# One value product for both head groups, and the softmax sums carried in the gathered tile

## The chip, the cores and the metric

The kernel runs on one core of a Trainium2 chip. The metric is device time in microseconds (us); the time of a kernel is the median of its runs. The profile is one execution taken by the hardware profiler. Engines: TensorE (PE; PEld is its weight load), VectorE (DVE), ScalarE (ACT), GpSimd (POOL), SyncE (SP, which issues nearly all loads here).

## The reference, cut to what matters

One decode step for 8 sequences: layer norm, attention over the last 1024 cached positions with 32 query heads on 8 key/value heads, a feed-forward branch that gates the result, and a residual.

```python
# B = 8, D = 512, Hq = 32, Hkv = 8, Sk = 4096, Dh = 128, W = 1024, F = 1792
xn = layernorm(x)
q = (xn @ wq) -> [B, Hq, 1, Dh]
k, v = k_cache[:, :, Sk-W:], v_cache[:, :, Sk-W:]    # 4 query heads share one kv head
p = softmax(q @ k.T * Dh**-0.5)
s = (p @ v).reshape(B, 1, Hq*Dh) @ wo
g = silu((gelu(xn @ w_gate) * (xn @ w_up)) @ w_down)
out = x + s * g
```

K and V of the window are 4.19 MB for one sequence (2.10 MB each), 33.6 MB of the 47.5 MB that the kernel reads.

## The kernel before, in words

The kernel is scheduled by hand: on each engine the instructions run in the order in which the program writes them. An instruction that waits for another engine holds up everything behind it on its own engine.

**Before the loop.** `wq` and the first K and V blocks are loaded; the layer norm is computed, `q` is projected (line 254) and spread into a block-diagonal stationary `qbd` (line 277). Constants are built: `sel` (line 213) selects, for one head group, the heads that belong to it; `neg_st` and `neg_mv` mask scores of foreign heads.

**Loads.** `slot` hands out eight slots of 16 KB a partition, each for one K or V block of one sequence, or for weights of the feed-forward and output projection. A load of a new block into a slot waits until the old one's last reader is done. Each block is loaded in two halves (line 83), one for each group of four kv heads (NG = 2). SyncE issues the loads in program order, with at most eight in flight: each waits for the landing of the eighth before it, besides its slot.

**The loop over the 8 sequences b** (lines 407 to 425) runs, in program order: loads of K for b+2 and V for b+1; `turn_k(b+1, 0)`; `softmax(b)`; `scores(b+1, 0)`; `gather(b-1)`; `turn_k(b+1, 1)`; `scores(b+1, 1)`; `turn_p(b)`; `values(b)`; `keep_o(b)`; and behind b = 4 `regroup(0)`.

- `turn_k(b, g)` (line 242): one transpose on VectorE in 32 x 32 blocks turns half of the K block into `kT`.
- `scores(b, g)` (lines 293 and 304): TensorE; for g = 0 first two mask matmuls, then 8 matmuls of 512 columns into `S`, [128 x 1024] in PSUM.
- `softmax(b)`: VectorE takes the maximum `mx` (line 314) and folds it twice (319, 321); ScalarE scales it into `nb` (324, four instructions) and takes the exponential into `P_sb` (326), whose accumulator writes the row sums to `sums[:, b]`.
- `turn_p(b)` (line 337): VectorE turns `P_sb` into `pT`.
- `values(b)` (line 348): TensorE, for each head group g 32 matmuls with 32 stationary columns and 128 moving columns of V. The chunk c goes to the column group t = c % 4, so that four partial sums for 32 heads lie on the 128 partitions of `O_ps`, [128 x 2 x 128].
- `keep_o(b)` (line 361): ScalarE copies `O_ps` to `O_sb`.
- `gather(b)` (lines 369 and 373): for each g one FP32 matmul with `sel` adds the four partial sums and picks the group's heads, into 128 columns of `o_ps`, and one more does the same with `sums[:, b]` into column 128.
- `regroup(q)` (lines 384 to 400), for four sequences at once: divide by the sums, spread, eight small matmuls `r_ps`, and a cast into `oT`.

**Behind the loop.** SyncE issues the loads of the feed-forward weights and `wo`; then `gather(7)`, `regroup(1)`, the gate and up matmuls `z_ps` and `u_ps` (459), GELU on ScalarE and VectorE (469 to 482), the down projection `f_ps` (488), the output projection `s_ps` (507, 128 matmuls in four blocks of 32, one for each megabyte of `wo`), and two VectorE instructions and a store for the result.

Of the kernel before, what the change touches and what calls it, by code (L numbers as in the profile page):

```python
# [11 lines left out]
FP32 = mybir.dt.float32  # L12
# [9 lines left out]
def kernel(  # L22
# [13 lines left out]
    nc = tc.nc  # L36

    B, Sq, D = A_x.shape
    Hkv, Sk, Dh = A_k_cache.shape[1], A_k_cache.shape[2], A_k_cache.shape[3]
# [6 lines left out]
    P = nc.NUM_PARTITIONS  # L46
    NK = D // P
    HG = 4
    NG = Hkv // HG
    C = W * HG // P  # L50
# [7 lines left out]
    keep = ctx.enter_context(tc.tile_pool(name="keep", bufs=1))  # L58
    two = ctx.enter_context(tc.tile_pool(name="two", bufs=2))
# [31 lines left out]
    k_sb, v_sb = {}, {}  # L91
# [4 lines left out]
    def load_v(b):  # L96
# [14 lines left out]
        out=ident,  # L111
        in_=ident,
# [13 lines left out]
        out=xpad,  # L126
        in_=xpad,
# [17 lines left out]
        out=xhat,  # L145
# [9 lines left out]
    with tc.tile_pool(name="ps_x", bufs=1, space=PSUM) as ps_x:  # L155
# [7 lines left out]
        for t in range(4):  # L163
# [4 lines left out]
                start=True,  # L168
                stop=True,
# [12 lines left out]
        out=hv,  # L182
        in_=hv,
# [7 lines left out]
        out=neg_st,  # L191
        in_=neg_st,
# [8 lines left out]
        out=neg_mv,  # L201
        in_=neg_mv,
# [10 lines left out]
    sel = consts.tile([P, NG, Hq], FP32, name="sel")  # L213
    nc.vector.memset(sel, 0.0)
    for g in range(NG):
        nc.vector.tensor_reduce(
            out=sel[:, g, g * qd : (g + 1) * qd],
            in_=ident.rearrange("p (t g h) -> p g h t", t=4, g=NG)[:, g],
# [5 lines left out]
        out=own, in_=ident.rearrange("p (i e) -> p e i", e=8), axis=AX.X, op=ALU.add  # L224
    )
    pick = consts.tile([P, 4 * NU], BF16, name="pick")
    with nc.allow_low_precision(reason="sums of zeros and a single one"):
        nc.vector.tensor_reduce(
            out=pick, in_=ident.rearrange("p (a e) -> p a e", e=8), axis=AX.X, op=ALU.add
# [20 lines left out]
    with tc.tile_pool(name="ps_q", bufs=1, space=PSUM) as ps_q:  # L250
        q_ps = [ps_q.tile([P, 512], FP32, name=f"q_ps{i}") for i in range(8)]
        for k in range(NK):
            for i in range(8):
# [4 lines left out]
                    start=(k == 0),  # L258
                    stop=(k == NK - 1),
# [19 lines left out]


    pT, S, P_sb, O_ps = {}, {}, {}, {}
    sums = keep.tile([P, B], FP32, name="sums")

    actx = ExitStack()
    ps_s = actx.enter_context(tc.tile_pool(name="ps_s", bufs=2, space=PSUM))
# [26 lines left out]
    def softmax(b):  # L312
        mx = two.tile([P, 1], FP32, name="mx")
        nc.vector.tensor_reduce(  # L314
            out=mx, in_=S[b].rearrange("p a c -> p (a c)"), axis=AX.X, op=ALU.max
        )

        m2 = two.tile([64, 1], FP32, name="m2")
        nc.vector.tensor_tensor(out=m2, in0=mx[0:64, :], in1=mx[64:128, :], op=ALU.max)
        m1 = two.tile([32, 1], FP32, name="m1")  # L320
        nc.vector.tensor_tensor(out=m1, in0=m2[0:32, :], in1=m2[32:64, :], op=ALU.max)  # L321
        nb = two.tile([P, 1], FP32, name="nb")
        for j in range(4):
            nc.scalar.mul(nb[32 * j : 32 * j + 32, :], m1, -inv)  # L324
        P_sb[b] = two.tile([P, C // 2, 32, 2], BF16, name="P_sb")
        nc.scalar.activation(  # L326
            out=P_sb[b].rearrange("p c i w -> p c w i"),
            in_=S[b].rearrange("p a (c w i) -> p (a c) w i", w=2, i=32),
            func=ACT.Exp,
            bias=nb,  # L330
            scale=inv,
            accum_out=sums[:, b : b + 1],
        )

    def turn_p(b):
        pT[b] = two.tile([P, C // 2, Hq, 2], BF16, name="pT")
        nc.vector.transpose(  # L337
            out=pT[b].rearrange("p c h w -> p (c h w)").bitcast(I32),
            in_=P_sb[b].rearrange("p c i w -> p (c i w)").bitcast(I32),
        )  # L340

    def values(b):
        O_ps[b] = ps_o.tile([P, NG, Dh], FP32, name="O_ps")
        for g in range(NG):
            vv = v_sb[b][:, g].rearrange("p (c d) -> p c d", d=Dh)
            for c in range(C):
                t = c % 4
                nc.tensor.matmul(  # L348
                    O_ps[b][32 * t : 32 * t + 32, g, :],
                    pT[b][:, c // 2, :, c % 2],  # L350
                    vv[:, c, :],
                    start=(c < 4),
                    stop=(c >= C - 4),
                )

    o_ps = {}
    O_sb = {}

    def keep_o(b):
        O_sb[b] = two.tile([P, NG, Dh], FP32, name="O_sb")  # L360
        nc.scalar.copy(out=O_sb[b], in_=O_ps[b])  # L361

    def gather(b):
        q = b % 4
        if q == 0:
            o_ps[b // 4] = ps_g.tile([P, Dh + 1], FP32, name="o_ps")
        o = o_ps[b // 4][32 * q : 32 * q + 32, :]
        for g in range(NG):
            nc.tensor.matmul(  # L369
                o[:, 0:Dh], sel[:, g, :], O_sb[b][:, g, :], start=(g == 0), stop=(g == NG - 1)  # L370
            )
        for g in range(NG):
            nc.tensor.matmul(
                o[:, Dh : Dh + 1],
                sel[:, g, :],
                sums[:, b : b + 1],
                start=(g == 0),
                stop=(g == NG - 1),
            )

    def regroup(q):

# [24 lines left out]
    for b in range(B):  # L407
        if b + 2 < B:
            load_k(b + 2)
        if b + 1 < B:  # L410
            load_v(b + 1)
            turn_k(b + 1, 0)
        softmax(b)
        if b + 1 < B:
            scores(b + 1, 0)
        if b >= 1:
            gather(b - 1)
        if b + 1 < B:
            turn_k(b + 1, 1)
            scores(b + 1, 1)  # L420
        turn_p(b)
        values(b)
        keep_o(b)
        if b == 4:
            regroup(0)
# [10 lines left out]
    for u in range(NU):  # L436
        if u % 2 == 0:
            pair = slot("wo_sb").rearrange("p (v j d) -> p v j d", v=2, d=D)
        t = pair[:, u % 2]
# [6 lines left out]
        wo.append(t)  # L446

    gather(B - 1)
    regroup(1)
    actx.close()  # L450
# [4 lines left out]
    for n, ws in (("z_ps", wgu[0]), ("u_ps", wgu[1])):  # L455
        ps = ps_f.tile([P, FT], FP32, name=n)
        for k in range(NK):
            for t in range(4):
# [4 lines left out]
                    start=(k == 0),  # L463
                    stop=(k == NK - 1),
# [6 lines left out]
        out=z2, in0=z2, scalar1=0.044715, scalar2=1.0, op0=ALU.mult, op1=ALU.add  # L471
# [11 lines left out]
        out=hT.rearrange("p j b -> p (j b)"), in_=h_bf.rearrange("p (y j) -> p j y", j=NJ)  # L483
    )
    f_ps = ps_f.tile([P, DT], FP32, name="f_ps")
    for j in range(NJ):
        for t in range(4):
# [4 lines left out]
                start=(j == 0),  # L492
                stop=(j == NJ - 1),
# [4 lines left out]
        out=g_sb, in0=g_sb, scalar1=0.5, scalar2=0.5, op0=ALU.mult, op1=ALU.add  # L498
# [5 lines left out]
    for u in range(NU):  # L504
        for j in range(8):
            for t in range(4):
# [4 lines left out]
                    start=(u == 0 and j == 0),  # L511
                    stop=(u == NU - 1 and j == 7),
# [7 lines left out]
        out=out_f.rearrange("b (t d) -> t b d", t=4), in_=out_sb[0 : P : RB, :]  # L520
# [31 lines left out]
```

## Time and profile before

| what | value |
|---|---|
| median of 3 runs | 121.2 us (121.13 to 121.26) |
| span of the profiled execution (first to last instruction) | 119.2 us |
| VectorE busy | 75.7 us, 63% of the span |
| TensorE busy | 70.9 us, 59% |
| ScalarE busy | 31.4 us, 26% |
| loads | 47.46 MB read, 398 GB/s over the span |
| value matmuls (line 348) | 512, 9.2 us busy |
| gather matmuls (line 369) | 32 rows, 5.4 us busy |
| exponential (line 326) | 8, 1390 ns each |
| `kT` transposes (line 242) | 16, 2286 ns each |

The span is the profiled execution's own time; no other time of that execution is given, and the runs' median is 2.0 us longer than it. In a row of the timeline the first number is the start in us from the span's start, the second the time until the end of the row, then engine, line, operation, output and inputs, their shapes and the count; in brackets is the idle time of the engine before it and what ended it. In the rows of 40 digits each digit is a fortieth of the span (2.98 us), in tenths; `PEclk` is the granted clock of TensorE, 9 being full.

### The profile page before, as it was taken

The numbers are of one execution on the slowest core, as the hardware profiler recorded it, in microseconds if no ns is written. First come the engines' busy times: TensorE is split into PE (matmuls) and PEld (weight loads), VectorE is DVE, ScalarE is ACT, GpSimd is POOL, SyncE is SP. The second block draws the span as 40 slices with busy tenths as digits, with TensorE's granted clock in tenths as the row PEclk, the third lists the DMA queues.
The fourth block names the chain that finished last, engine by engine and source line by source line (L and its number), as shares of the span: only waits on it lengthen the run. The fifth ranks groups of instructions, "written<-read, shape, count | busy, mean of one in ns | idle before, by whom it ended". The sixth has DMA issues, their size and how long they took to land.

```text
span 119.2 us, 2306 instructions
## 1 busy us (share of the span) xinstructions
PE 70.9 (59%) x992; PEld 37.9 (32%) x992; DVE 75.7 (63%) x101; ACT 31.4 (26%) x75; POOL 3.2 (3%) x10
## 2 busy tenths in 40 slices
PE   0000079971299498896969692875783547544370
PEld 0000033420034154453635451433452433143350
DVE  1000387969998999999999968949952241751000
ACT  0300240076500715144161700421618101100000
POOL 2000052000000000000000000000000000000000
PEclk9999999998559999999999999999999755555555
DMA  6898899999999999999999999999999999999930
GB/s 177 352 518 363 374 429 432 423 429 426 434 418 423 434 426 421 426 432 418 423 432 426 421 423 429 423 429 421 423 429 433 443 438 404 438 414 429 402 140 3
DMA packets 6110, 47.61 MB, mean 399 GB/s; under 512 B 716, under 2 KB 852, under 8 KB 1108
## 3 DMA queue, kind: packets, MB, share of 16 engines
q1 hardware_dynamic: 6084, 47.46, 94.7%
q8 instruction: 8, 0.13, 0.4%
q14 instruction: 2, 0.02, 0.0%
q10 hardware_dynamic: 16, 0.01, 0.0%
HBM read 47.46 MB, written 0.01 MB: 398 GB/s over the span
## 4 chain that ended last, share of the span: by engine, by line
DMA 78%; PE 9%; DVE 6%; ACT 2%; issue 1%; ACTq 1%; DVEq 0%; SPq 0%
DMA k_sb<-in_A_k_cache_dram 32%; DMA wo_sb<-in_A_wo_dram 20%; DMA v_sb<-in_A_v_cache_dram 16%; DMA x_sb<-in_A_x_dram 9%; PE q_ps L254 8%; DVE qbd L277 3%; ACTq L78 1%; DVE q_both L267 1%; ACT L154 1%; DVE q_both L264 1%; PE s_ps L507 1%; DVE stats L137 1%; DVE y L515 0%; ACT rstd L141 0%; DVE out_sb L517 0%
## 5 line engine op out<-in xcount | busy, mean ns | idle before, releaser
L304 PE MATMUL S_ps<-kT,qbd 128*128 128x512 bf16 x128 | 31.9, 393 | 14.8 <-DVE kT L242 11.3
L242 DVE STREAM_TRANSPOSE kT<-k_sb 128x2048 int32<-128x2048 int32 x16 | 36.5, 2286 | 1.6 <-DMA k_sb<-in_A_k_cache_dram 1.6
L304 PEld LDWEIGHTS <-qbd 128*128 128x128 bf16 x128 | 12.6, 99 | 30.8 <-issue 14.2
L324 ACT ACTIVATE nb<-m 32x1 f32<-32x1 f32 x32 | 6.4, 201 | 20.1 <-DVE m L321 19.8
L326 ACT ACTIVATE P_sb<-S_ps,nb 128x1024 bf16<-128x1024 f32 x8 | 11.1, 1390 | 0.3
L348 PE MATMUL O_ps<-v_sb,pT 128*32 128x128 bf16 x512 | 9.2, 227 | 2.6 <-DVE pT L337 2.6
L314 DVE TENSOR_REDUCE mx<-S_ps 128x1 f32<-128x1024 f32 x8 | 9.6, 1194 | 1.6 <-PE S_ps L304 1.6
L254 PE MATMUL q_ps<-wq_sb,xnR 128*128 128x512 bf16 x32 | 9.9, 485 | 0.5 <-ACT x_res L171 0.5
L348 PEld LDWEIGHTS <-pT 128*32 128x32 bf16 x512 | 7.7, 100 | 5.6 <-issue 3.0
L159 PE MATMUL xnT_ps<-ident,xhat 8*128 8x8 bf16 x4 | 0.3, 174 | 15.2 <-DVE xhat L144 15.2
L361 ACT COPY O_sb<-O_ps 128x256 f32<-128x256 f32 x8 | 3.0, 372 | 22.7 <-PE O_ps L348 22.7
L137 DVE BATCH_NORM_STATS2 stats<-x_sb 8x6 f32<-8x512 bf16 x1 | 0.7, 681 | 12.0 <-DMA x_sb<-in_A_x_dram 12.0
L337 DVE STREAM_TRANSPOSE pT<-P_sb 128x512 int32<-128x512 int32 x8 | 5.7, 711 | 3.4 <-ACT P_sb L326 3.3
L507 PE MATMUL s_ps<-wo_sb,oT 128*32 128x128 bf16 x128 | 4.4, 307 | 3.9 <-DMA wo_sb<-in_A_wo_dram 3.9
L369 PE MATMUL o_ps<-O_sb,sel 128*32 128x128 f32 x32 | 5.4, 297 | 0.9 <-ACT O_sb L361 0.9
L293 PE MATMUL S_ps<-neg_mv,neg_st 128*128 128x512 bf16 x16 | 4.8, 381 | 1.9 <-DVE q_both L264 1.9
L254 PEld LDWEIGHTS <-xnR 128*128 128x128 bf16 x32 | 3.8, 118 | 6.4 <-issue 3.9
L264 ACT CAST q_both<-q_ps 128x512 bf16<-128x512 f32 x6 | 3.0, 613 | 8.6 <-PE q_ps L254 8.6
L507 PEld LDWEIGHTS <-oT 128*32 128x32 bf16 x128 | 3.5, 136 | 4.9 <-issue 4.7
L159 PEld LDWEIGHTS <-xhat 8*128 8x128 bf16 x4 | 0.2, 113 | 15.2 <-DVE xhat L144 15.2
L515 DVE TENSOR_TENSOR y<-s_ps,g_sb 128x128 f32<-128x128 f32 x1 | 0.3, 292 | 7.4 <-PE s_ps L507 7.4
L369 PEld LDWEIGHTS o_ps<-O_sb,sel 128*32 128x32 f32 x32 | 3.0, 115 | 4.0 <-issue 2.5
(64 smaller groups left out, 53.9 us busy)
## 6 DMA issues: line engine op xcount, KB each, us to landing
k_sb<-in_A_k_cache_dram SPq DMA_DIRECT2D x16, 1024.0 KB, 16.5
v_sb<-in_A_v_cache_dram SPq DMA_DIRECT2D x16, 1024.0 KB, 19.8
wq_sb<-in_A_wq_dram SPq DMA_DIRECT2D x1, 4096.0 KB, 12.2
wo_sb<-in_A_wo_dram SPq DMA_DIRECT2D x3, 1024.0 KB, 25.0
wgu_sb<-in_B_w_gate_dram SPq DMA_DIRECT2D x1, 1792.0 KB, 21.3
wgu_sb<-in_B_w_up_dram SPq DMA_DIRECT2D x1, 1792.0 KB
wd_sb<-in_B_w_down_dram SPq DMA_DIRECT2D x1, 1792.0 KB
wo_sb<-in_A_wo_dram SPq DMA_DIRECT2D x1, 640.0 KB
```

The lines of the kernel that those rows point to most:

```text
L242: nc.vector.transpose(out=t.bitcast(I32), in_=k_sb[b][:, g].bitcast(I32))
L254: nc.tensor.matmul(q_ps[i], xnR[:, k, :, :].rearrange("p j b -> p (j b)"), wq_sb[k][:, i * 512 : (i + 1) * 512], start=(k == 0), stop=(k = ...
L264: e(out=q_bf[:, i * 512 : (i + 1) * 512], in_=q_ps[i])
L293: nc.tensor.matmul(S[b][:, half, :], neg_st.rearrange("p j h -> p (j h)"), neg_mv.rearrange("p a n -> p (a n)"), start=True, stop=False,)
L304: nc.tensor.matmul(S[b][:, half, :], qbd[:, m, b, w, g, :], kv[:, half * 16 : (half + 1) * 16, m, :, w], start=False, stop=(g == NG - 1 an ...
L314: nc.vector.tensor_reduce(out=mx, in_=S[b].rearrange("p a c -> p (a c)"), axis=AX.X, op=ALU.max)
L324: nc.scalar.mul(nb[32 * j : 32 * j + 32, :], m1, -inv)
L326: nc.scalar.activation(out=P_sb[b].rearrange("p c i w -> p c w i"), in_=S[b].rearrange("p a (c w i) -> p (a c) w i", w=2, i=32), func=ACT.Exp,
L337: nc.vector.transpose(out=pT[b].rearrange("p c h w -> p (c h w)").bitcast(I32), in_=P_sb[b].rearrange("p c i w -> p (c i w)").bitcast(I32),)
L348: nc.tensor.matmul(O_ps[b][32 * t : 32 * t + 32, g, :], pT[b][:, c // 2, :, c % 2], vv[:, c, :], start=(c < 4), stop=(c >= C - 4),)
L369: nc.tensor.matmul(o[:, 0:Dh], sel[:, g, :], O_sb[b][:, g, :], start=(g == 0), stop=(g == NG - 1))
L507: nc.tensor.matmul(s_ps[32 * t : 32 * t + 32, :], oT[:, j, u, :], wo[u][:, j, t * DT : (t + 1) * DT], start=(u == 0 and j == 0), stop=(u = ...
```

## The change

The value products of both head groups become one matmul for each chunk c: 32 matmuls with 256 moving columns (two runs of 128, one from each half of the V block) in place of 64 with 128. `O_sb` becomes [128 x 2 x 129]. It is allocated in `softmax(b)`, ahead of the exponential, whose accumulator now writes the row sums into column 128 of group 0; a VectorE copy of one column puts them into column 128 of group 1. `keep_o` writes columns 0 to 127 of both groups. `gather` then is one matmul of 129 columns for each group, and `sums` and its own two matmuls go. In VectorE's order the new copy stands behind the two folds of the maximum (319, 321) and ahead of `turn_k(b+1, 1)`. Loads and their order are the same.

```diff
-    sums = keep.tile([P, B], FP32, name="sums")
...
         P_sb[b] = two.tile([P, C // 2, 32, 2], BF16, name="P_sb")
+        O_sb[b] = two.tile([P, NG, Dh + 1], FP32, name="O_sb")
         nc.scalar.activation(
...
-            accum_out=sums[:, b : b + 1],
-        )
+            accum_out=O_sb[b][:, 0, Dh : Dh + 1],
+        )
+        nc.vector.tensor_copy(out=O_sb[b][:, 1, Dh : Dh + 1], in_=O_sb[b][:, 0, Dh : Dh + 1])
...
     def values(b):
         O_ps[b] = ps_o.tile([P, NG, Dh], FP32, name="O_ps")
-        for g in range(NG):
-            vv = v_sb[b][:, g].rearrange("p (c d) -> p c d", d=Dh)
-            for c in range(C):
-                t = c % 4
-                nc.tensor.matmul(
-                    O_ps[b][32 * t : 32 * t + 32, g, :],
-                    pT[b][:, c // 2, :, c % 2],
-                    vv[:, c, :],
-                    start=(c < 4),
-                    stop=(c >= C - 4),
-                )
+        vv = v_sb[b].rearrange("p g (c d) -> p c g d", d=Dh)
+        for c in range(C):
+            t = c % 4
+            nc.tensor.matmul(
+                O_ps[b][32 * t : 32 * t + 32, :, :],
+                pT[b][:, c // 2, :, c % 2],
+                vv[:, c, :, :],
+                start=(c < 4),
+                stop=(c >= C - 4),
+            )
...
     def keep_o(b):
-        O_sb[b] = two.tile([P, NG, Dh], FP32, name="O_sb")
-        nc.scalar.copy(out=O_sb[b], in_=O_ps[b])
+        nc.scalar.copy(out=O_sb[b][:, :, 0:Dh], in_=O_ps[b])
...
         for g in range(NG):
-            nc.tensor.matmul(
-                o[:, 0:Dh], sel[:, g, :], O_sb[b][:, g, :], start=(g == 0), stop=(g == NG - 1)
-            )
-        for g in range(NG):
-            nc.tensor.matmul(
-                o[:, Dh : Dh + 1],
-                sel[:, g, :],
-                sums[:, b : b + 1],
-                start=(g == 0),
-                stop=(g == NG - 1),
-            )
+            nc.tensor.matmul(o, sel[:, g, :], O_sb[b][:, g, :], start=(g == 0), stop=(g == NG - 1))
```

## The prediction, made before the changed kernel ran

> **What bounds the kernel now.** I read the page first: the DMA row, the chain, the clock row.
>
> ```profile
> span 119.2 us, 2306 instructions
> DVE  1000387969998999999999968949952241751000
> PEclk9999999998559999999999999999999755555555
> DMA  6898899999999999999999999999999999999930
> DMA 78%; PE 9%; DVE 6%; ACT 2%; issue 1%; ACTq 1%; DVEq 0%; SPq 0%
> ```
>
> Loads are busy without a gap to slice 37, and the chain that ended last runs through them. VectorE is full as well, but mainly in slices 9 to 22 (27 to 69 us): there it works through K blocks that have already landed. At 80.68 it waits for a load (`k_sb`) for the only time in the attention loop. The end waits for `wo`: in the timeline of TensorE,
>
> ```profile
> 105.90 1.69 PE L488 MATMUL f_ps<-wd_sb,hT 128*32 128x128 bf16 x56 [2.72 <-DVE hT L482]
> 108.17 1.04 PE L507 MATMUL s_ps<-wo_sb,oT 128*32 128x128 bf16 x32 [0.58 <-DMA wo_sb<-in_A_wo_dram]
> ...
> 114.66 1.23 PE L507 MATMUL s_ps<-wo_sb,oT 128*32 128x128 bf16 x32 [0.50 <-DMA wo_sb<-in_A_wo_dram]
> ```
>
> Each of the four blocks of `s_ps` sits idle until its weights land. Without those waits the blocks would follow `f_ps` at once: 105.90 + 1.69 + 4 x 0.9 (a block's 1.04 less its fill) = 111.2, where 115.9 is measured. So compute may come 4.7 us later at no cost. Beyond that, each microsecond counts in full, because gather, regroup, feed-forward and `s_ps` are a serial tail behind the last softmax. Everything then hangs on one pass of the loop, VectorE first, ScalarE after it (b = 1):
>
> ```profile
> 44.30 1.19 DVE L314 TENSOR_REDUCE mx<-S_ps 128x1 f32<-128x1024 f32 x1
> 45.52 0.15 DVE L319 TENSOR_TENSOR m<-mx 64x1 f32<-64x1 f32 x1
> 45.71 0.15 DVE L321 TENSOR_TENSOR m<-m 32x1 f32<-32x1 f32 x1
> 45.79 2.29 DVE L242 STREAM_TRANSPOSE kT<-k_sb 128x2048 int32<-128x2048 int32 x1
> 48.23 0.71 DVE L337 STREAM_TRANSPOSE pT<-P_sb 128x512 int32<-128x512 int32 x1 [0.15 <-ACT P_sb L326]
> 48.87 2.27 DVE L242 STREAM_TRANSPOSE kT<-k_sb 128x2048 int32<-128x2048 int32 x1
> ```
>
> ```profile
> 45.89 0.84 ACT L324 ACTIVATE nb<-m 32x1 f32<-32x1 f32 x4 [1.19 <-DVE m L321]
> 46.76 1.39 ACT L326 ACTIVATE P_sb<-S_ps,nb 128x1024 bf16<-128x1024 f32 x1
> 48.02 0.18 ACT L326 ACTIVATION_READ_ACCUMULATOR P_sb<-S_ps,nb 128x1 f32 x1
> ```
>
> The `kT` transpose at 45.79 runs while ScalarE does bias and exponential: VectorE has 2.29 us of work for a 2.37 us absence, and idles 0.15. A pass takes 51.06 - 44.30 = 6.76 us.
>
> **The added copy.** The new `tensor_copy` of the sums stands in program order behind the maxima and ahead of `turn_k(b+1, 1)`, and it reads what the exponential's accumulator writes. So VectorE waits until 48.23 before it may begin the transpose that used to fill that time. Counted from the start M of `mx`: copy at +3.93; 0.10 for the copy (no row has it; from 0.08, the pitch between line 321 and the next start, to 0.16, that of the reciprocal at 69.15 on the same 128x1; I take the nearer to the first, as nothing waits on its result at once); transpose +4.03 to +6.32; `turn_p` one pitch of 2.20 later, +6.23; `turn_k(b+2, 0)` 0.64 later, +6.87; the next `mx` 2.19 later, +9.06. Its scores are done before that: 1.99 us after the transpose ends (86.69 to 88.68 in b = 6), +8.31. A pass grows from 6.76 to 9.06, by 2.30.
>
> Who waits for it: `scores(b+1, 1)` on TensorE needs this transpose, and the values follow. Pass by pass: b = 0 to 3 cost 4 x 2.30 = 9.2. Pass 4 (regroup; 64.58 to 74.42, 9.84) continues from the transpose's end through `scores`, `values`, `r_ps` and the cast to the next `mx`, so it moves with that end, from +3.78 to +6.32: 2.54. Pass 5 took 74.42 to 82.91, 8.49, with its load wait in it; 9.06 takes its place: 0.57. Pass 6 has no further K block and ends with its scores: 2.54. The last pass has only the copy itself, 0.10. Sum 14.95.
>
> **The matmuls taken away.** Values go from 64 matmuls of 128 columns to 32 of 256 in each batch. They take 1.08 us at full clock, four column groups side by side; halving the weight loads may save up to 0.3 and a strided operand may cost as much, and I take nothing: in the loop they lie ahead of `scores(b+2, 0)`, which will have some 3 us to spare. In the tail, at half clock, they take 1.64 (93.41), and the same columns stream; 0, from -0.3 to +0.3. The gather drops the four one-column matmuls. In the loop it is hidden; in the tail they end at 96.74 where the other four end at 96.58, so 0.16 goes, at most 0.37, for one more column; I take -0.2. `keep_o` now writes rows of 129, the same 256 elements; 0 for its 0.37, hidden in the loop, one copy in the tail, 0 to 0.1.
>
> `O_sb` is now taken at the exponential, with two buffers: it waits for `gather(b-2)`, which TensorE did ahead of the scores that the exponential reads anyway. Nothing.
>
> **Loads.** Releases of slots come later. The worst is `wo`: its first load needs `turn_k(6, 1)`. With `mx` of batch 5 at 37.50 + 4 x 9.06 + (9.84 + 2.54) = 86.1 it issues at 92.4 instead of 83.13, the second pair after `values(5)`, 6.37 + 1.83 + 1.08 = 9.3 behind that `mx`, 95.4. With the longest time from issue to landing of a `wo` load, 25.0, that lands at 120.4; the first `s_ps` needs it at 122.3 (below). K and V loads issue at most about 2.5 later, with 16.5 to 19.8 us of queue ahead of them. I take nothing, though only by that margin.
>
> **The clock.** TensorE's gap changes. In passes 1 to 3 it now waits 0.93 us for `kT`. After the change `values(b)` ends 0.2 behind the next M, mask, scores and gather follow for 3.0, and `scores(b+1, 1)` starts at +6.37: a gap of 3.1 to 3.2. The windows show what gaps do:
>
> ```profile
> 30.00:32.00 2.00, 0.00 (x0) 0.00 (x0) 1.97 (x7) 1.50 (x3) 0.00 (x0) 0.50 1.01 426
> 71.00:75.00 4.00, 1.80 (x37) 1.05 (x26) 3.06 (x3) 0.37 (x1) 0.00 (x0) 1.00 1.02 424
> 93.00:94.00 1.00, 0.59 (x36) 0.59 (x40) 0.35 (x1) 0.00 (x0) 0.00 (x0) 0.87 0.90 387
> 94.00:95.00 1.00, 1.00 (x40) 0.78 (x32) 0.00 (x0) 0.00 (x0) 0.00 (x0) 0.50 0.97 416
> ```
>
> The seventh number is the granted clock. A gap of 2.20 (to 74.55) left it at 1.00; 2.56 (to 93.41) ended at 0.50; after the gap to 32.04 it came back within 4 us of work (0.64 in the window 35 to 36, 1.00 next). So 3.1 can halve it, not always. At half clock the 8 score matmuls take 1.83 more, of which 0.75 (+8.31 to +9.06) is covered: 1.08 a cold pass, 1.83 in passes 4 and 6. Behind a cold stretch comes contiguous work that restores it, so I take three of the seven passes at about 0.95 (the last of the eight may already be fast): +2.8, from 0 to 5 x 1.08 + 2 x 1.83 = 9.1.
>
> [...]
>
> **Sum.** The start of `z_ps`: 98.92 + 14.95 - 0.2 = 113.7; `f_ps` 6.98 later, `s_ps` at 122.3, without waits for `wo`. Span 119.2 + 14.75 - 4.7 + 2.8 = 132.1. The runs' median is 121.2, 2.0 over the profiled span, which I keep: 134.0.
>
> **Rivals.**
> A, the forecast: one to five cold passes, 132 to 137.
> B, no pass cold: the gap stays harmless as the 2.20 one was; 131.2.
> E, the clock also full in the tail, where it is 0.50 now: halves of values (0.6), gather (0.5), `z_ps` (0.8), `f_ps` (0.8) and `s_ps` (1.8) go, 131.2 - 4.5 = 126.7. Against it, the tail keeps gaps of 2.5 and 2.7 us.
> C, all seven passes cold: 131.2 + 9.1 = 140.3. Against it, each cold pass runs without a gap for several us.
> D, not slower: loads still set the end, because VectorE's loop stays inside the 4.7 us. A batch brings 4.19 MB, about 9.8 us at 428 GB/s, longer than 9.06, so VectorE could wait for loads instead. This decides if the wait adds under 0.6 us a pass. Against it, VectorE waits on loads only in pass 5, and starts the loop with landed blocks in hand, so its 2.30 is not taken out of idle time. 121.2.
>
> **Chances.** A 0.67, B 0.14, C 0.10, E 0.06, D 0.03. The range 129.5 to 138.5 takes in A and B with the bounds of the small terms (copy, values, `keep_o`: about 1.5) and leaves out C, D and E, 0.19. A difference under 0.2% (0.24 us) cannot be told from none here: D splits into 0.02 for that and 0.01 for faster.
>
> **What would show it.** Right: the copy on VectorE with some 2.3 us idle before it, released by ScalarE; `turn_p` without a wait; a pass of 9.1 to 10.1; `mx` of the last batch near 103.5 to 107; no idle before `s_ps` for `wo`; loads ending near 115 as now. Wrong: the copy issued after the transpose, or VectorE waiting for K loads in most passes, or a load row with gaps, or `s_ps` still waiting for weights.

## The result and the profile after

The changed kernel takes 136.1 us (median of 6 runs, 134.3 to 137.1) against 121.2 us. The ratio is 1.114 (95% interval 1.111 to 1.118) by the three runs within 1.5% of the fastest, whose median is 135.0, and 1.123 by the median of all six. The profiled execution took 134.34 us, with a span of 132.5.

The rows of the page that answer to those shown of before, in slices of 3.31 us:

```profile
span 132.5 us, 1742 instructions
DVE  1000779999944954954955946683972812256411
PEclk9999999995599689689779779999869859995559
DMA  5989999999999999999999999999999999800000
PE 37%; DVE 31%; ACT 17%; DMA 8%; issue 3%; ACTq 1%; DVEq 0%
```

The loads still run without a gap, and they end in slice 34, near 115 us as before. But they are off the chain that ended last: their share falls from 78% to 8%. TensorE, VectorE and ScalarE have taken their place, one after the other. VectorE's row has a valley in each pass, and the granted clock now drops in most passes of the loop.

One pass of VectorE in the timeline, b = 1, from `mx` to the next `mx`:

```profile
47.54 1.22 DVE L313 TENSOR_REDUCE mx<-S_ps 128x1 f32<-128x1024 f32 x1 [0.75 <-PE S_ps L303]
...
51.51 0.15 DVE L334 COPY O_sb<-O_sb 128x1 f32<-128x1 f32 x1 [2.38 <-ACT P_sb L326]
51.58 2.30 DVE L242 STREAM_TRANSPOSE kT<-k_sb 128x2048 int32<-128x2048 int32 x1
53.80 0.67 DVE L338 STREAM_TRANSPOSE pT<-P_sb 128x512 int32<-128x512 int32 x1
54.40 2.27 DVE L242 STREAM_TRANSPOSE kT<-k_sb 128x2048 int32<-128x2048 int32 x1
57.45 1.23 DVE L313 TENSOR_REDUCE mx<-S_ps 128x1 f32<-128x1024 f32 x1 [0.79 <-PE S_ps L303]
```

The copy of one column takes 0.15 us, but VectorE stands still for 2.38 us in front of it, until ScalarE's exponential has written its sums. The `kT` transpose that used to run in that time starts behind it, and `turn_p` no longer waits. The pass takes 9.91 us instead of 6.76. Its last 0.79 is a second wait: `mx` now waits for the scores. TensorE's timeline shows why. Before, the second group of scores of this pass waited 0.93 us for its `kT` and took 1.90:

```profile
48.13 1.90 PE L304 MATMUL S_ps<-kT,qbd 128*128 128x512 bf16 x8 [0.93 <-DVE kT L242]
```

After, the same group of this pass, that of pass 4, and the end:

```profile
53.94 3.48 PE L303 MATMUL S_ps<-kT,qbd 128*128 128x512 bf16 x8 [2.61 <-DVE kT L242]
...
82.93 1.91 PE L303 MATMUL S_ps<-kT,qbd 128*128 128x512 bf16 x8 [2.19 <-DVE kT L242]
...
124.05 1.69 PE L477 MATMUL f_ps<-wd_sb,hT 128*32 128x128 bf16 x56 [4.08 <-DVE hT L471]
125.52 3.63 PE L496 MATMUL s_ps<-wo_sb,oT 128*32 128x128 bf16 x128
```

The same eight matmuls take 3.48 us behind a gap of 2.61 and 1.91 behind one of 2.19: the first ran at half clock (the granted clock is 0.51 from 54 to 57 us and 1.00 from 83 to 85). The 128 matmuls of `s_ps` follow `f_ps` in one row, with no wait for `wo`.

### The profile page after: what moved, and what is told of

Same layout as the page of the kernel before. It is cut to its first block, busy times and chain, and to the rows that moved or that the text cites. A ratio compares the mean times of both kernels' runs of the same rounds, so it can differ in the third digit from the quotient of the medians.

```text
span 132.5 us, 1742 instructions
## 1 busy us (share of the span) xinstructions
PE 75.6 (57%) x697; PEld 35.5 (27%) x704; DVE 76.2 (58%) x109; ACT 31.2 (24%) x75; POOL 3.2 (2%) x10
## 4 chain that ended last, share of the span: by engine, by line
PE 37%; DVE 31%; ACT 17%; DMA 8%; issue 3%; ACTq 1%; DVEq 0%
PE S_ps L303 21%; DVE kT L242 13%; ACT P_sb L326 9%; DMA x_sb<-in_A_x_dram 8%; PE q_ps L254 6%; DVE mx L313 6%; ACT nb L323 5%; PE O_ps L348 4%; PE s_ps L496 3%; DVE qbd L277 2%; PE f_ps L477 1%; ACTq L78 1%; DVE q_both L267 1%; DVE o_x L375 1%; ACT L154 1%
## 5 line engine op out<-in xcount | busy, mean ns | idle before, releaser
L303 PE MATMUL S_ps<-kT,qbd 128*128 128x512 bf16 x128 | 41.3, 480 | 26.4 <-DVE kT L242 22.7
L303 PEld LDWEIGHTS <-qbd 128*128 128x128 bf16 x128 | 14.4, 113 | 48.3 <-issue 35.9
L334 DVE COPY O_sb<-O_sb 128x1 f32<-128x1 f32 x8 | 1.2, 154 | 19.4 <-ACT P_sb L326 19.4
L348 PE MATMUL O_ps<-v_sb,pT 128*32 128x256 bf16 x256 | 9.7, 300 | 2.7 <-DVE pT L338 2.7
L254 PE MATMUL q_ps<-wq_sb,xnR 128*128 128x512 bf16 x32 | 8.8, 445 | 0.5 <-ACT x_res L171 0.5
L348 PEld LDWEIGHTS <-pT 128*32 128x32 bf16 x256 | 6.6, 106 | 8.8 <-DVE kT L242 3.1
L368 PE MATMUL o_ps<-O_sb,sel 128*32 128x129 f32 x32 | 5.0, 279 | 1.0 <-ACT O_sb L360 1.0
L292 PE MATMUL S_ps<-neg_mv,neg_st 128*128 128x512 bf16 x9 | 3.4, 392 | 2.0 <-DVE q_both L264 2.0
L477 PE MATMUL f_ps<-wd_sb,hT 128*32 128x128 bf16 x56 | 1.7, 312 | 4.1 <-DVE hT L471 4.1
L245 DVE MEMSET qbd<- 128x4096 uint32 x1 | 3.5, 3472 | 0.8 <-issue 0.8
```

Source lines behind the costliest of these rows:

```text
L245: nc.vector.memset(qbd, 0.0)
L254: nc.tensor.matmul(q_ps[i], xnR[:, k, :, :].rearrange("p j b -> p (j b)"), wq_sb[k][:, i * 512 : (i + 1) * 512], start=(k == 0), stop=(k = ...
L292: nc.tensor.matmul(S[b][:, half, :], neg_st.rearrange("p j h -> p (j h)"), neg_mv.rearrange("p a n -> p (a n)"), start=True, stop=False,)
L303: nc.tensor.matmul(S[b][:, half, :], qbd[:, m, b, w, g, :], kv[:, half * 16 : (half + 1) * 16, m, :, w], start=False, stop=(g == NG - 1 an ...
L348: nc.tensor.matmul(O_ps[b][32 * t : 32 * t + 32, :, :], pT[b][:, c // 2, :, c % 2], vv[:, c, :, :], start=(c < 4), stop=(c >= C - 4),)
L368: nc.tensor.matmul(o, sel[:, g, :], O_sb[b][:, g, :], start=(g == 0), stop=(g == NG - 1))
```

## The experiments

The theory: the place of the copy in VectorE's queue is the loss, in two parts, the wait itself and the half clock that TensorE's longer gap brings. The rivals: the new matmuls cost something, the longer passes come from elsewhere, or slower loads do it.

**e1: the copy later.** The changed kernel with the copy at the head of `turn_p`, behind the transpose.

```diff
-        nc.vector.tensor_copy(out=O_sb[b][:, 1, Dh : Dh + 1], in_=O_sb[b][:, 0, Dh : Dh + 1])
...
     def turn_p(b):
+        nc.vector.tensor_copy(out=O_sb[b][:, 1, Dh : Dh + 1], in_=O_sb[b][:, 0, Dh : Dh + 1])
```

> The changed kernel with its one-column copy moved behind the second kT transpose, at the head of turn_p, where VectorE waits for ScalarE anyway (0.15 us a pass before the change). Theory (the copy's place in VectorE's queue is the whole loss): the loop returns to passes of 6.8 to 6.9 us, the end waits for wo again, 121.2 us, 120.9 to 121.6. Rival (the 256-column matmuls or the 129-column gather cost the time): stays near 134 to 137.

Measured 123.05 us, 1.016 times before (1.014 to 1.017). The passes are back at 6.82 us, and `s_ps` waits for `wo` again. That is 13.1 of the 14.9 us, but 1.9 us remain that neither side expected. They are in the loads. In the windows, the last number is the rate in GB/s; the kernel before:

```profile
30.00:80.00 50.00, 39.13 (x492) 20.06 (x492) 45.79 (x48) 16.81 (x44) 0.00 (x0) 0.94 1.01 426
```

and e1:

```profile
30.00:80.00 50.00, 40.62 (x311) 18.37 (x312) 45.23 (x51) 15.90 (x42) 0.00 (x0) 0.90 1.01 418
```

The queues are as busy (1.01), but move 1.9% less. The changed kernel shows 419. e5, e6 and e9 follow this up.

**e2: the wait alone.** The kernel before, with one dummy copy in the change's place.

```diff
+    extra = keep.tile([P, B], FP32, name="extra")
...
             accum_out=sums[:, b : b + 1],
         )
+        nc.vector.tensor_copy(out=extra[:, b : b + 1], in_=sums[:, b : b + 1])
```

> The kernel before, with one added VectorE copy of one column of sums into a tile that nobody reads, in the place where the change has its copy; values and gather as before. Theory (the wait alone makes the loss): passes of 9.1 to 10, time 134 to 138. Rival (the new matmuls and gather make part of it): under 131.

Measured 137.14 us, 1.131 (1.128 to 1.133). Values and gather are the old ones, and the whole loss is there:

```profile
60.43 0.15 DVE L335 COPY extra<-sums 128x1 f32<-128x1 f32 x1 [2.37 <-ACT P_sb L327]
60.50 2.30 DVE L242 STREAM_TRANSPOSE kT<-k_sb 128x2048 int32<-128x2048 int32 x1
```

One thing besides the wait is in this run: the tile `extra` (32 bytes a partition) moves the load slots, and the loads run at 419 GB/s, as in the changed kernel. e6 prices that by itself, and e10 shows that it costs nothing at this length.

**e3: the values alone.** The kernel before, with the new `values` and nothing else.

```diff
-        for g in range(NG):
-            vv = v_sb[b][:, g].rearrange("p (c d) -> p c d", d=Dh)
...
+        vv = v_sb[b].rearrange("p g (c d) -> p c g d", d=Dh)
...
```

> The kernel before, with the value products as 32 matmuls of 256 columns and nothing else changed. Theory: off the path in the loop, and the end waits for wo: 121.2 us, 120.9 to 121.5, values 0.9 to 1.1 us a batch at full clock. Rival (fewer weight loads shorten the kernel): under 120.9; rival (the strided moving operand costs): values over 1.3 us a batch, time still near 121.2 because of the 4.7 us of slack.

Measured 121.08 us, 0.9995 (0.9987 to 1.0004): no difference. The 32 matmuls of 256 columns take 1.06 us at full clock where 64 of 128 took 1.08; at half clock both take 1.90 (at 93.22 here, at 114.71 in e2).

**e4: the gap filled.** The changed kernel with zeros multiplied into the open score sums while TensorE would be idle.

```diff
+    zero = keep.tile([P, P], BF16, name="zero")
+    nc.gpsimd.memset(zero, 0.0)
...
+    def fill(b):
+        for i in range(12):
+            nc.tensor.matmul(
+                S[b][:, i % 2, :],
+                zero,
+                neg_mv.rearrange("p a n -> p (a n)"),
+                start=False,
+                stop=False,
+            )
...
             turn_k(b + 1, 1)
+            fill(b + 1)
             scores(b + 1, 1)
```

> The changed kernel with 12 matmuls of zeros into the open score accumulation, ahead of each second group of scores, so that TensorE has 2.75 us of work in its gap (the result is the same). Theory (TensorE's gap halves the clock in most passes and that costs about 5 us in the loop): no score group at half clock, passes of 9.1, mx of the last batch near 103.6 instead of 108.7, time 129 to 132. Rival (the longer passes have another cause, or the filler itself holds up the scores): 134 or more.

Measured 129.95 us, 1.072 (1.068 to 1.076): 6.2 us less than the changed kernel, with 84 matmuls more (in the profiled executions 129.53 against 134.34, 4.8 less). In the windows the number behind the five engines is the granted clock:

```profile
38.00:60.00 22.00, 19.73 (x147) 9.04 (x146) 14.69 (x18) 7.49 (x20) 0.00 (x0) 1.00 1.01 418
60.00:84.00 24.00, 21.33 (x185) 10.04 (x184) 17.46 (x20) 5.62 (x15) 0.00 (x0) 1.00 1.01 418
```

It stays at 1.00 from 38 to 84 us, where the changed kernel shows valleys, and four of the five passes in it take 9.02 to 9.05 us (the fifth has regroup). From the first `mx` to the last it is 65.8 us, against 71.0 in the changed kernel: 5.2 us of the loop were half clock. The second groups of scores are all at 1.9:

```profile
61.15 1.90 PE L305 MATMUL S_ps<-kT,qbd 128*128 128x512 bf16 x8 [0.60 <-DVE kT L244]
```

One first group (85.31, behind regroup, where nothing fills the gap) was still at half clock in most of it (3.16 us, at a granted clock of 0.58), at no cost.

**e5: the slots moved to a multiple of 64 bytes.** The change takes the 32 bytes of `sums` from ahead of the load slots, but it also makes each of the two buffers of `O_sb` 8 bytes longer, and the built program places the two 1056 bytes apart, 1024 before: 64 more, less 32. In the kernel before, the slots begin at multiples of 2048 bytes of a partition; in the changed kernel and e1, 32 bytes past one. e5 is e1 with 32 unused bytes in front, which puts them 64 past.

```diff
+    pad = keep.tile([P, 8], FP32, name="pad")
+    nc.gpsimd.memset(pad, 0.0)
     x_sb = keep.tile([B, D], BF16, name="x_sb")
```

> e1 with an unused tile of 32 bytes a partition put in front, so that the load slots start at a multiple of 64 bytes again, as in the kernel before (with the change the tile of sums, 32 bytes, is gone from ahead of them, and they start 32 bytes off). Theory (e1's 1.9 us are slower loads, 418 against 426 GB/s, by where the slots start): loads at 425 to 427 GB/s between 30 and 80 us, 121.1 us, 120.8 to 121.4. Rival (the copy or the new gather costs the 1.9 us): 122.9 to 123.1.

Measured 122.59 us, 1.013 (1.011 to 1.015), and 420 GB/s: hardly better. By itself this left both open: a multiple of 64 is not enough, or it is not the start of the slots.

**e6: the kernel before, moved by 32 bytes.** The same two lines in the kernel before.

```diff
+    pad = keep.tile([P, 8], FP32, name="pad")
+    nc.gpsimd.memset(pad, 0.0)
```

> The kernel before, with an unused tile of 32 bytes a partition ahead of the slots and no other edit. Theory (slot start): loads at 418 to 419 GB/s between 30 and 80 us, 122.9 to 123.1 us. Rival (slot start does not matter): 121.1.

Measured 122.80 us, 1.014 (1.013 to 1.016), at 418 GB/s. An unused tile is enough to cost the kernel before 1.8 us, which speaks for the place of the slots; e9 tests which places are good. (The tiles that e2 and e4 add move the slots too, to 32 and 288 bytes past a multiple of 2048, and both ran at 419 GB/s.)

**e9: the slots at a multiple of 256 bytes.** e1 with a tile of 56 floats in front.

```diff
+    pad = keep.tile([P, 56], FP32, name="pad")
+    nc.gpsimd.memset(pad[:, 0:8], 0.0)
```

> e1 with an unused tile of 224 bytes a partition put in front, so that the load slots start at a multiple of 256 bytes (but not of 512); before they start at a multiple of 2048, in e1 32 and in e5 64 bytes past one of those. Theory (slot starts off a multiple of 256 bytes slow each load; a multiple of 64 was not enough): loads at 425 to 427 GB/s between 30 and 80 us, 121.0 us, 120.7 to 121.3. Rival (a coarser multiple is wanted, or something else in e1 slows the loads): 122.4 to 123.1 and 418 to 420 GB/s. [...]

Measured 121.03 us, 0.9988 (0.9979 to 0.9996), and the rate is back:

```profile
30.00:80.00 50.00, 38.78 (x324) 18.22 (x328) 45.83 (x53) 16.49 (x44) 0.00 (x0) 0.97 1.01 426
```

Starts 32 and 64 bytes past a multiple of 2048 ran at 418 and 420 GB/s, those 256 past at 426: the rates fell by 1.9 and 1.4%, so the start 32 past cost more than the one 64 past. Why is not shown, and no start between 64 and 256 was tried. This is the change with its copy in the right place; it is 0.1% faster than the kernel before by the interval, below the 0.2% that this case can tell.

**e7 and e8: the early copy in some passes.** e5 with the copy in the change's place for b = 2 and 3 (e7) and for b = 0 to 3 (e8), and late in the others. They test the slack: how much delay of the loop is free. Their measure is e5, 122.59 us.

```diff
         nc.scalar.activation(
...
+        if b in (2, 3):        # e8: (0, 1, 2, 3)
+            nc.vector.tensor_copy(out=O_sb[b][:, 1, Dh : Dh + 1], in_=O_sb[b][:, 0, Dh : Dh + 1])
...
     def turn_p(b):
-        nc.vector.tensor_copy(out=O_sb[b][:, 1, Dh : Dh + 1], in_=O_sb[b][:, 0, Dh : Dh + 1])
+        if b not in (2, 3):
+            nc.vector.tensor_copy(out=O_sb[b][:, 1, Dh : Dh + 1], in_=O_sb[b][:, 0, Dh : Dh + 1])
```

> e5 with the copy in the change's early place for b = 2 and 3 only. Theory (a delay of the loop is free up to the wait for a load in pass 5, 1.6 us, and the 4.7 us of slack before s_ps): two passes of 9.1 to 10, the delay of 4.5 to 6.5 us taken up, 121.0 to 121.6 us. Rival (each wait of VectorE reaches the end): 125.5 to 127.5.

Measured 122.49 us, 1.012 (1.011 to 1.014): two waits cost nothing. The two passes took 9.96 and 9.52 us, and the last `mx` starts at 92.37 instead of 90.01. The first half of `s_ps` no longer waits, the rest still does:

```profile
111.18 1.93 PE L501 MATMUL s_ps<-wo_sb,oT 128*32 128x128 bf16 x64
114.52 0.63 PE L501 MATMUL s_ps<-wo_sb,oT 128*32 128x128 bf16 x32 [1.41 <-DMA wo_sb<-in_A_wo_dram]
```

> e5 with the copy in the change's early place for b = 0 to 3. Theory: a delay of 9 to 12 us, less 1.6 and 4.7: 2.7 to 5.9 us over 121.1, so 123.8 to 127. Rival (each wait reaches the end): 130 to 133. Rival (loads hide it all): 121.1.

Measured 125.99 us, 1.041 (1.039 to 1.043), 3.4 us over e5. The last `mx` starts at 99.23, 9.2 later than in e5 (1.3 of it because the loop began later), and the wait for `wo` is gone:

```profile
117.34 3.63 PE L501 MATMUL s_ps<-wo_sb,oT 128*32 128x128 bf16 x128
```

5.8 of the 9.2 us were free, which is about the 4.7 of the prediction and some 1.3 by which the loads end later in e5 than before (its last block of `s_ps` starts at 116.00, before at 114.66).

**e10: the change itself at a multiple of 512 bytes.**

```diff
+    pad = keep.tile([P, 120], FP32, name="pad")
+    nc.gpsimd.memset(pad[:, 0:8], 0.0)
```

> The changed kernel, copy in its early place, with an unused tile of 480 bytes ahead of the slots, so that they start at a multiple of 512 bytes. Theory (in the changed kernel the loads end some 15 us ahead of the last instruction, so their rate does not count there): loads at 425 to 427 GB/s, last landing near 112 to 114, and the time stays at 134 to 137.5. Rival (a share of the loss comes through slower loads): under 134.

Measured 135.92 us, 1.126 (1.121 to 1.130): the rate is 426 again, and the time lies within the 134.3 to 137.1 of the changed kernel. In this kernel, where loads do not set the end, 419 instead of 426 GB/s does not count.

## Why the prediction was right, and where its terms were off

The forecast was 134.0 us, 129.5 to 138.5; measured were 136.1, and 134.34 in the profiled execution. Direction and mechanism held:

- **The wait.** Expected 2.3 us of idle time ahead of the copy; it is 2.37 to 2.38 in all passes but one. The copy's own pitch is 0.07 (51.51 to 51.58), for 0.10. e2 shows that this instruction makes the whole loss with the old values and gather, e9 that the rest of the change costs nothing where the slots start at a multiple of 256 bytes.
- **The pass at full clock.** Expected 9.06; e4 shows 9.02, and 65.8 us from the first `mx` to the last where the prediction's passes make 66.0.
- **The slack.** Expected 4.7 us before `s_ps` and 1.6 us in pass 5: e7 stays within it and e8 goes beyond it. In the changed kernel no block of `s_ps` waits for `wo`.
- **Late slots.** `wo` is issued at 95.3 where 92.4 was expected, and the loads end near 115 without making anyone wait. The margin of 1.9 us was not needed: the slowest `wo` load took 16.1 us from issue to landing, where the prediction allowed 25.0.
- **Values and gather.** 0 and -0.2 were taken; the 0.3 allowed either way for the weight loads and the strided operand was the author's estimate, of which e3 shows 0.02 (1.06 for 1.08); the gather at half clock takes 1.07 (97.59 in e1) for 1.22. The 1.64 us that the prediction read as values at half clock (93.41) were so in part only, 0.87 being the clock from 93 to 94; wholly at half clock they take 1.90.

One sign missed: the `mx` of the last batch was expected at 103.5 to 107 and started at 108.68. Two terms were mis-sized, and in the profiled execution they cancel, which is luck:

- **Half clock in the loop: 2.8 taken, 5.0 measured.** The step that counted "three of the seven passes" failed. The passes took 9.87, 9.91, 9.61, 9.05, 12.83, 9.81 and 9.93 us; against 9.06, 12.38 and 8.31 that is 0.8, 0.9, 0.6, 0, 0.5, 0.8 and 1.6 over. Six of the seven second score groups ran at half clock in part or whole, where rival A said one to five; an ordinary pass with such a group cost 0.6 to 0.9, near the 0.95 taken, so the count was wrong more than the price. That contiguous work restores the clock was right (the first score group, the next in line, is at 1.90 in each of the passes), but the next gap took it away again. The gap of 3.1 to 3.2 us that the prediction counted on appears only behind a pass at full clock (3.16 at 62.86 in e2); behind a slow group the gather ends later, and 2.6 were left, which still sufficed. The 0.5 of pass 4 is a path that the prediction lacked: its own scores were in time, but the values behind them ran at half clock (75.94, 1.90 us), so ScalarE's `keep_o` ended late, and the bias of the next softmax, behind it in ScalarE's queue, started at 78.16 instead of some 0.1 us behind the fold at 77.52 + 0.15. The copy waited 2.83 instead of 2.38.
- **The tail: 1.9 us less than taken.** It was priced at half clock, as before. In this execution the clock was full until about 119: from the last `mx` to `z_ps` 9.14 instead of 10.14, from there to `f_ps` 6.23 instead of 6.98, and to the end of `s_ps` 5.10 instead of 5.29. That is part of rival E.

Together: 132.1 + 2.2 - 1.9, and 0.2 for a loop that started later, is 132.6, and the span is 132.5. The other runs were longer, and the granted clock goes with the time: 0.858 in the profiled run, 0.844 at 135.03, 0.820 at 137.14. So does most of the spread of 2.8 us, against 0.2 before. The profiled execution of e2, 135.4 long, had the luck on neither side: 72.9 us from the first `mx` to the last, 6.9 over the full-clock 66.0, and values (114.71) and `z_ps` at half clock in the tail.

Rival B (no pass at half clock) would have been 131.2; e4, which makes that condition, took 129.95. Rival C (each pass) was nearer in the number of slow groups, but its price, 9.1, is further from the measured 5.0 than the 2.8 of the forecast. Rival D needed under 0.6 us a pass; it is 2.3.

Not foreseen at all: that the change moves the load slots by 32 bytes and slows the loads by 1.9% (418 against 426 GB/s in e1). In the changed kernel this costs nothing (e10). Had the copy stood in the right place, the same step of the prediction, "Loads", would have been wrong by 1.9 us.

## What to carry to other kernels

An instruction of 0.15 us can cost as much as the wait in front of it (2.38 us here), when the work queued behind it used to fill that wait: place it behind that work, where its engine waits anyway. Ask then what the longer pass does to the other engines: gaps of 2.2 to 4.3 us on TensorE, one in each pass, cost another 5 us of the loop here, and useless matmuls in the gap won it back (71.0 us from the first `mx` to the last without them, 65.8 with them). And where loads set the end, look at where their buffers start after any tile ahead of them changes its size (418 to 420 GB/s against 426 here).

## What the runs showed of the hardware

**The clock and gaps.** In these traces the length of the gap alone does not decide. In the changed kernel the clock was halved about when work resumed after 2.57 (63.85) and 2.61 us (53.94, 105.15), within 1.1 us after one of 2.26 (73.46: 2.55 us for the eight), and stayed full after 2.41 (89.07) and 2.70 us (113.47):

```profile
63.85 3.17 PE L303 MATMUL S_ps<-kT,qbd 128*128 128x512 bf16 x8 [2.57 <-DVE kT L242]
73.46 2.55 PE L303 MATMUL S_ps<-kT,qbd 128*128 128x512 bf16 x8 [2.26 <-DVE kT L242]
89.07 1.90 PE L303 MATMUL S_ps<-kT,qbd 128*128 128x512 bf16 x8 [2.41 <-DVE kT L242]
113.47 1.06 PE L348 MATMUL O_ps<-v_sb,pT 128*32 128x256 bf16 x32 [2.70 <-DVE pT L338]
```

The 16 changes of the granted clock in its trace from 30.17 to 129.16 us lie 3.41 us or two, three or five times that apart, those of the kernel before (28.89, 35.71, 93.74) two and seventeen times.

What separates the cases is where the gap lies on the grid of 3.41 us that these changes mark. In the traces of these two kernels, cut into windows at that grid from 15 us on: at full clock, each of the 9 windows in which TensorE was busy for 1.28 us or less was followed by half clock, and each of the 29 with 1.85 us or more by full clock; of the five in between, 1.55 to 1.84 us, four were followed by full clock and one by half. At half clock, each of the 9 windows with 3.15 us or more brought the full clock back, and none of the 11 with 2.53 or less. The gaps of 2.57 and 2.61 us each lay inside one window and left it 0.80 to 0.84 us of work; the one of 2.70 was cut by the boundary at 112.09, and its two windows had 1.61 and 1.55.

Three windows are 10.24 us, close to a pass of 9.9, and windows at half clock begin at 43.82, 54.06, 64.30 and 74.54: the gaps of four passes in a row fell inside a window each, until a boundary at 81.37 cut the one that ends at 82.93. That would be why three slow passes were too few; it is read from the trace, and no run varied the length of the pass to test it.

**The start of a load's destination.** Loads of 1 MB into slots at multiples of 2048, 512 or 256 bytes ran at 426 GB/s, into slots 64 bytes past at 420, and 32 past at 418 to 419, in rows of 8 KB a partition. The price was 1.6 to 1.9 us of a kernel that reads 47.5 MB.
